# A clustered-attention and MoE kernel: spreading 1/sum over rows by float16 products of two halves, and a planner that holds an engine for shorter waits

## The chip, the core and the metric

The kernel runs on one core of a Trainium2 chip. The core has engines with a queue of their own each: TensorE (PE for the products, PEld for the loading of their stationary operand), VectorE (DVE), ScalarE (ACT), GpSimd (POOL), and SyncE (SP), which issues the transfers here. Each works through its queue in order and waits on semaphores of the others. The metric is the device time of one execution in microseconds (us); less is better.

## The reference

Queries, keys and values of 4 batches, 8 heads, 768 positions and 64 columns. Each query and each key is given to the nearest of 16 centroids of its head, and a query sees only keys of its own cluster. The output of the attention goes through two matrices with a gate between them.

```python
q_assign = np.argmax(np.einsum('bhsd,hcd->bhsc', q_n, c_n), axis=-1)
k_assign = np.argmax(np.einsum('bhsd,hcd->bhsc', k_n, c_n), axis=-1)
mask = q_assign[:, :, :, None] == k_assign[:, :, None, :]
scores = np.where(mask, scale * np.matmul(q, k.transpose(0, 1, 3, 2)), -1000000000.0)
scores = scores - np.max(scores, axis=-1, keepdims=True)
attn = np.exp(scores)
attn = attn / (np.sum(attn, axis=-1, keepdims=True) + 1e-09)
x = np.matmul(attn, v)                       # then (B*S, H*D) = 3072 x 512
h = x @ w_in                                 # 512 x 2048
g = np.where(h >= 1, h, np.where(h <= -1, 0.0, (h + 1) ** 2 / 4))
out = g @ w_out                              # 2048 x 512
```

## The kernel before

Numbers are kept as two float16 halves, a high one and what is left over; a product of two such numbers is three float16 products (high·high, high·low, low·high) that add up in PSUM.

The work is cut into units: a batch, a pair of heads and a chunk of 256 queries, 4 × 4 × 3 = 48 of them. For a unit, `at_scores` runs four times (two heads, two blocks of 128 queries): four products of 384 columns on TensorE into `bank`, and one VectorE instruction that adds a mask value and takes the row's bound into `sS` and `sbi`. `at_soft` takes the exponential on ScalarE with the row sum in `rs`, splits it into the halves `hl` (ScalarE makes the high one, POOL subtracts it for the low one), and SP issues the transpose of `hl` to `pT`. After the fourth (`n == 3`) ScalarE copies the four sums with 1e-9 added, and VectorE takes the reciprocal `rr`.

`at_av` (lines 758 to 791) is one group of instructions on TensorE. It fills one half of the PSUM tile `banka` with 1/sum, each number spread over 64 rows and its query's column: four products of a broadcast column of `rr` with the float32 identity `idf`, 128 columns wide. The other half gets the 36 products of `pT` with the values, 256 columns wide. Both heads of the pair stand side by side: their products use 64 columns of the array each. ScalarE then copies the 1/sum half to `rb`, VectorE multiplies, and ScalarE and POOL split the result into the halves of `x` (in some units the tile's name is `wk`).

`ffn1` and `ffn2` are the two matrix products for 256 rows of x; their steps on the other engines are named `r` and `g`. Ahead of it all, keys, queries and values are loaded, scaled, split and transposed (`kv_scale`, `kq_split`, `v_split`), each batch gets a bound of its values (`v_bound`, `v_am`), centroid products give the clusters (`assign`, products named `<-cT`), and the weights are scaled and split (`w_bits`, `w_sum`, `w_split`; the products `<-wk,ones`).

None of this is issued as it is written. `Recorder` collects all instructions as nodes with their dependencies, and `issue` (line 274) plans the order: `forward` runs a model of the engines with the prices of `price`, `backward` makes priorities from it, eight rounds are made, and the order of the round with the shortest modelled end is issued. Nearly every instruction therefore has line 289 in the profile. In `forward`, an engine normally takes the instruction that is ready and has the best priority. Lines 182 to 188 make the exception: where another instruction becomes ready within `LOOK` times the price of the chosen one, and has a priority better by more than `MARGIN` ns, the engine waits for that.

```python
more = [(s, r, i) for r, s, i in q[:8] if r < t + x.cost * LOOK and s < pick[0] - MARGIN]
if more:
    heappush(avail[e], pick)
    _, t, i = min(more)
```

Of the kernel before, what the change touches and what calls it, by code (L numbers as in the profile page):

```python
# [9 lines left out]
F16 = mybir.dt.float16  # L10
BF16 = mybir.dt.bfloat16
F32 = mybir.dt.float32
U32 = mybir.dt.uint32
AF = mybir.ActivationFunctionType
ALU = mybir.AluOpType
# [5 lines left out]


ONE, ES_MIN = 65504.0, 2.0**-23
EXP_MASK2 = 0x7F000000
TINY = 2.0**-47
W_TINY = 2.0**-90
# [2 lines left out]
LATENCY = dict(tensor=280, scalar=252, vector=230, gpsimd=175)  # L29
COLD, AHEAD = 75e3, 1500  # L30

LOOK, MARGIN = 1.0, 3000
ROUNDS = 8


# [312 lines left out]
def tile_clustered_attention_moe(  # L348
# [10 lines left out]
    nc = tc.nc  # L359
    B, H, S, D = q.shape  # L360
    C = cent.shape[1]
# [4 lines left out]
    P = 128  # L366
    T = S // P
    NP = H // 2
    CT = 2
# [18 lines left out]
    rec = Recorder(tc)  # L388
# [48 lines left out]
    rings["c"] = Ring([rings["sS"].bufs[1][:, i * D : (i + 1) * D] for i in range(3)])  # L437
    rings["c_hl"] = Ring([rings["sS"].bufs[2]])
    make_identity(nc, idf)
    iota = const.tile([P, C], F32, name="iota")  # L440
    for c in range(C):
        nc.gpsimd.memset(iota[:, c : c + 1], float(C - c))
    zero = const.tile([P, 1], F32, name="zero")
    nc.gpsimd.memset(zero, 0.0)
    onh = const.tile([P, P], F16, name="onh")
    nc.gpsimd.memset(onh, 1.0)
    ones = const.tile([P, P], BF16, name="ones")
    nc.gpsimd.memset(ones, 1.0)
    cst = new("c", [D], F32)
# [122 lines left out]
    def assign(b, hp):  # L572

        e = KV[b, hp]
        n2 = 2 * T
        n4 = 2 * n2
        z1 = misc(n4, C)
        for i, x in enumerate("kq"):
            with rec.group():
                for n in range(n2):  # L580
                    h = 2 * hp + n // T
                    for a in range(2):
                        rec.tensor.matmul(
                            z1[:, i * n2 + n],
                            e[x + "T"][:, n],
                            cT[:, a, h * C : (h + 1) * C],
                            start=(a == 0),
                            stop=(a == 1),
                        )
        mx = new("mx", [n4], F32)  # L590

        def wide(x):
            return x.unsqueeze(2).to_broadcast([P, n4, C])


        rec.vector.tensor_reduce(out=mx, in_=z1, op=ALU.max, axis=AX.X)
        rec.vector.tensor_tensor(out=z1, in0=z1, in1=wide(mx), op=ALU.is_equal)
        rec.vector.tensor_tensor(out=z1, in0=z1, in1=iota.unsqueeze(1).to_broadcast([P, n4, C]), op=ALU.mult)
        rec.vector.tensor_reduce(out=mx, in_=z1, op=ALU.max, axis=AX.X)
        rec.vector.tensor_tensor(out=z1, in0=z1, in1=wide(mx), op=ALU.subtract)  # L600

        rec.gpsimd.memset(e["kn"][:, :, 0, C:], 0.0)
        for i, x in enumerate("kq"):
            rec.vector.tensor_scalar(
                out=e[x + "n"][:, :, 0, :C],
                in0=z1[:, i * n2 : (i + 1) * n2],
                scalar1=0.0,
                scalar2=-ONE if x == "k" else ONE,
                op0=ALU.not_equal if x == "k" else ALU.is_equal,
                op1=ALU.mult,  # L610
            )

        kn, qn = e["kn"], e["qn"]
        rec.gpsimd.tensor_tensor(
            out=kn[:, :, 1], in0=kn[:, :, 1], in1=e["phi"].unsqueeze(2).to_broadcast([P, n2, D]), op=ALU.mult
        )
        kf = e["kT"].rearrange("p n q -> p (n q)")
        rec.scalar.activation(out=kf, in_=kf, func=AF.Copy, scale=e["phi"])
        qf = e["q"].rearrange("p j (t d) -> p (j t) d", d=D)
        rec.scalar.activation(out=qn[:, :, 1], in_=qf, func=AF.Copy, scale=e["sc"][:, 1:2])  # L620
        for x, part in (("k", 3), ("q", 2)):
            e[x + "1"] = view(e["parts"][part], [n2, P], F16)
            transpose(e[x + "1"], e[x + "n"])

        pn = misc(2, C)
        with rec.group():
            for t in range(T):
                rec.tensor.matmul(pn, onh, kn[:, t::T, 0, :C], start=(t == 0), stop=(t == T - 1))
        has = new("has", [2, C], F32)
        rec.vector.tensor_scalar(out=has, in0=pn, scalar1=-ONE * (S - 0.5), scalar2=None, op0=ALU.is_gt)  # L630

        zq = z1[:, n2:].rearrange("p (j t) c -> p j t c", j=2)
        rec.vector.tensor_tensor(out=zq, in0=zq, in1=has.unsqueeze(2).to_broadcast([P, 2, T, C]), op=ALU.add)
        zm = z1[:, :n2, 0]
        rec.vector.tensor_reduce(out=zm, in_=z1[:, n2:], op=ALU.max, axis=AX.X)
        er = e["er"] = new("er", [n2], F32, NP)
        rec.vector.tensor_scalar(out=er, in0=zm, scalar1=e["es"], scalar2=None, op0=ALU.mult)
# [97 lines left out]
    def at_soft(b, hp, c, j, t):  # L735
        e = A.setdefault((b, hp, c), {})
        n = j * CT + t
        sS, bi = A.pop((b, hp, c, j, t))
        if n == 0:
            e["rs"] = new("rs", [4], F32, 4)  # L740
        if t == 0:
            e["pT", j] = new("pT", [2 * T, CT, P], F16, 3)
        sf = sS.rearrange("p a s -> p (a s)")
        rec.scalar.activation(
            out=sf, in_=sf, func=AF.Exp, bias=bi, scale=-1.0, accum_out=e["rs"][:, n : n + 1]
        )
        hl = new("hl", [2, S], F16, 3)
        rec.scalar.copy(hl[:, 0], sf)
        rec.gpsimd.tensor_tensor(out=hl[:, 1], in0=sf, in1=hl[:, 0], op=ALU.subtract)
        rec.sync.dma_start_transpose(out=e["pT", j][:, :, t, :], in_=hl.rearrange("p a s -> p (a s)"))  # L750
        if n == 3:

            rr = new("rr", [4], F32, 3)
            rec.scalar.activation(out=rr, in_=e["rs"], func=AF.Copy, bias=1e-9)
            rec.vector.reciprocal(rr, rr)
            e["rr"] = rr

    def at_av(b, hp, c):
        u = b * NCH + c
# [2 lines left out]
        pv, rb = bank_a[:, :CQ], bank_a[:, CQ:]  # L762
        with rec.group():
            for t in range(CT):
                for j in range(2):
                    rec.tensor.matmul(
                        rb[j * D : (j + 1) * D, t * P : (t + 1) * P],
                        e["rr"][:, j * CT + t : j * CT + t + 1].to_broadcast([P, D]),
                        idf,
                        start=True,  # L770
                        stop=True,
                    )
            for kc in range(T):
                for i, (va, pa) in enumerate(((0, 0), (0, 1), (1, 0))):
                    for j in range(2):
                        pT = e["pT", j].rearrange("p (a n) t q -> p a n (t q)", a=2)[:, pa, kc]
                        rec.tensor.matmul(
                            pv[j * D : (j + 1) * D],
                            kv["vs"][:, va, j, kc * D : (kc + 1) * D],
                            pT,  # L780
                            start=(kc == 0 and i == 0),
                            stop=(kc == T - 1 and i == 2),
                        )
# [272 lines left out]
```

## Time and profile before

| | us |
|---|---|
| median of three runs | 966.27 |
| lowest and highest of them | 966.08, 966.28 |
| the execution that was profiled | 964.51 |
| its span, first to last instruction | 962.7 |
| mean granted clock of TensorE | 0.976 |

The profile is of one execution. Its page has the busy time of each engine, the span in 40 slices, the chain of work that ended last, and the costliest groups of instructions. The views that are quoted below also give the timeline of one engine, the groups with their shapes kept apart, the waits by who waited for whom, and busy times in chosen windows. A timeline row has the start, the length, the engine, the source line, the operation, output and inputs, and in brackets the idle time just before it with what ended it. In a group's row stand count, busy time, mean ns of one, and idle time before them.

### The profile page before, as it was taken

The page shows a single profiled execution, that of the slowest core. Times are in us where ns is not written, and L with a number is a line of the kernel's source. Part 1 is how long each engine was busy: PE and PEld are TensorE (multiplying, and loading weights), DVE is VectorE, ACT ScalarE, POOL GpSimd, SP SyncE. Part 2 cuts the span into 40 slices and gives each one's busy share as a digit, 9 for nine tenths or more (in the row PEclk, how much of TensorE's full clock was granted, in tenths as well). Part 3 has the DMA queues.
Part 4 walks back from the last instruction along what each step waited for, and adds up shares of the span by engine and source line. Part 5 has one row for each costly group of instructions (what it writes and reads, how often), then busy time and mean ns, then how long its engine had stood idle before and what let it go on. Part 6 is the DMA issues. An engine that isn't in the chain of part 4 may idle for free.

```text
span 962.7 us, 19220 instructions
## 1 busy us (share of the span) xinstructions
PE 824.1 (86%) x7348; PEld 567.2 (59%) x7348; DVE 639.8 (66%) x1341; ACT 654.8 (68%) x1095; POOL 551.2 (57%) x421
## 2 busy tenths in 40 slices
PE   0335547878999999998988999999989999999998
PEld 0223335555666766675656766776666757767664
DVE  6998986878689865556778665546986554454231
ACT  3676877775667877765767687757777677676332
POOL 1375777574555767663655667656655666656311
PEclk9999779989999999999999999999999999999999
DMA  9998787778589986876789878867999776566100
GB/s 279 263 202 195 175 207 161 164 175 194 125 176 178 169 141 117 170 148 142 173 154 198 145 156 152 166 130 159 209 192 154 139 132 122 108 118 110 34 22 22
DMA packets 426780, 148.68 MB, mean 154 GB/s; under 512 B 403520, under 2 KB 418880, under 8 KB 426688
## 3 DMA queue, kind: packets, MB, share of 16 engines
q1 hardware_dynamic: 426688, 147.46, 75.7%
q8 instruction: 57, 0.93, 0.4%
q14 instruction: 35, 0.29, 0.1%
HBM read 40.40 MB, written 6.29 MB: 49 GB/s over the span
## 4 chain that ended last, share of the span: by engine, by line
PE 67%; DVE 22%; issue 5%; ACT 2%; POOL 2%; DMA 1%; SPq 0%; ACTq 0%; DVEq 0%; POOLq 0%
PE bank L289 47%; PE banka L289 12%; PE bankh L289 9%; DVE w L289 4%; DVE sS L289 4%; DVE bank L289 2%; DVE r L289 2%; DVE wk L289 1%; DVE am L289 1%; DVE qn L289 1%; DVE kn L289 1%; POOL hl L289 1%; DVE kvq L289 1%; DVE mx L289 1%; DMA kvq<-in_v_dram 1%
## 5 line engine op out<-in xcount | busy, mean ns | idle before, releaser
L289 POOL TENSOR_TENSOR hl<-sS,hl 128x768 f16<-128x768 f32 x192 | 330.4, 1725 | 182.5 <-ACT hl L289 103.6
L289 PE MATMUL bank<-w,g 128*128 128x512 f16 x1152 | 273.1, 383 | 0.5 <-DVE o L289 0.5
L289 PEld LDWEIGHTS <-kvq 128*64 128x64 f16 (+1 forms) x3264 | 195.4, 107 | 128.3 <-issue 80.8
L289 PEld LDWEIGHTS <-w 128*128 128x128 f16 x2304 | 224.5, 98 | 66.7 <-issue 25.5
L289 DVE CUSTOM_DVE_ANT_0 sS<-bank,zero,er 128x768 f32<-128x768 f32 x192 | 194.2, 1012 | 93.1 <-PE bank L289 77.0
L289 ACT ACTIVATE sS<-sS,sbi 128x768 f32<-128x768 f32 x192 | 179.2, 933 | 98.8 <-DVE sbi L289 92.8
L289 PE MATMUL bank<-kvq 128*128 128x384 f16 x768 | 164.1, 338 | 47.5 <-DVE sbi L289 42.0
L289 POOL TENSOR_TENSOR g<-r,g 128x512 f16<-128x512 f32 x96 | 115.2, 1200 | 152.7 <-ACT g L289 139.5
L289 PEld LDWEIGHTS <-g 128*128 128x128 f16 x1152 | 111.0, 98 | 122.8 <-issue 10.1
L289 ACT CAST hl<-sS 128x768 f16<-128x768 f32 x192 | 157.4, 825 | 7.4 <-DMA pT<-hl 5.6
L289 PE MATMUL bank<-x,w 128*128 128x256 f16 x1032 | 125.6, 275 | 10.0 <-DVE r L289 4.4
L289 ACT ACTIVATE r<-r,f_ra,f_rs 128x512 f32<-128x512 f32 x96 | 77.8, 811 | 79.4 <-DVE r L289 74.7
L289 PE MATMUL banka<-pT,kvq 128*64 128x256 f16 x1728 | 108.0, 281 | 0.0
L289 DVE TENSOR_SCALAR r<-bank,f_lo,f_hi 128x512 f32<-128x512 f32 x64 | 51.7, 808 | 61.6 <-PE bank L289 45.4
L289 ACT CAST g<-r 128x512 f16<-128x512 f32 x96 | 58.8, 613 | 31.7 <-DVE r L289 24.8
L289 DVE SCALAR_TENSOR_TENSOR r<-bank,f_gs,r 128x512 f32<-128x512 f32 x64 | 48.0, 749 | 30.9 <-ACT r L289 18.7
L289 PE MATMUL bank<-wk,w 128*128 128x256 f16 x504 | 60.1, 272 | 5.9 <-DVE r L289 4.9
L289 PE MATMUL bankh<-x,w 128*128 128x256 f16 x504 | 59.9, 273 | 0.2 <-DVE es L289 0.2
L289 DVE TENSOR_SCALAR r<-bankh,f_lo,f_hi 128x512 f32<-128x512 f32 x32 | 25.9, 809 | 30.8 <-PE bankh L289 24.8
L289 PEld LDWEIGHTS <-ones 128*128 128x128 bf16 x148 | 13.9, 120 | 50.5 <-issue 46.7
L289 POOL TENSOR_TENSOR w<-w 128x1024 f16<-128x1024 f32 x14 | 31.5, 2252 | 14.7 <-ACT w L289 14.7
L289 PE MATMUL bank<-wk,ones 128*128 128x128 bf16 x116 | 13.2, 277 | 29.8 <-DVE wk L289 29.8
(135 smaller groups left out, 840.1 us busy)
## 6 DMA issues: line engine op xcount, KB each, us to landing
w<-in_moe_w_in_dram SPq DMA_DIRECT2D x14, 512.0 KB, 4.9
w<-in_moe_w_out_dram SPq DMA_DIRECT2D x14, 512.0 KB, 4.3
kvq<-in_k_dram SPq DMA_DIRECT2D x16, 384.0 KB, 4.0
kvq<-in_q_dram SPq DMA_DIRECT2D x16, 384.0 KB, 3.7
kvq<-in_v_dram SPq DMA_DIRECT2D x16, 384.0 KB, 4.1
out_dram<-o SPq DMA_DIRECT2D x11, 512.0 KB, 3.4
pT<-hl SPq DMA_TRANSPOSE x192, 4.1
o<-in_v_dram SPq DMA_DIRECT2D x8, 384.0 KB, 3.9
```

The costliest lines, as they stand in the source:

```text
L289: fn(*args, **kw)
```

## The change

1/sum is split into two float16 halves. ScalarE scales the sum by 2^-10 ahead of the reciprocal, in place in `rs`; POOL converts the reciprocal (a CAST to `rr`) and subtracts (the second half of `rr`). `at_av` has eight float16 products where it had four of float32: high and low half after one another into the same place. Their moving operand is `idu`, an identity that is scaled by 2^-10, made once on POOL. The ones of float16 (`onh`) go, and `assign` uses those of bfloat16. In the planner LOOK goes from 1.0 to 0.4 and MARGIN from 3000 to 4000.

```diff
+UNIT = 2.0**-10
...
-LOOK, MARGIN = 1.0, 3000
+LOOK, MARGIN = 0.4, 4000
...
     make_identity(nc, idf)
+    idu = const.tile([P, P], F16, name="idu")
+    rec.gpsimd.tensor_scalar(out=idu, in0=idf, scalar1=UNIT, scalar2=None, op0=ALU.mult)
...
-    onh = const.tile([P, P], F16, name="onh")
-    nc.gpsimd.memset(onh, 1.0)
...
-                rec.tensor.matmul(pn, onh, kn[:, t::T, 0, :C], start=(t == 0), stop=(t == T - 1))
+                rec.tensor.matmul(pn, ones, kn[:, t::T, 0, :C], start=(t == 0), stop=(t == T - 1))
...
-            rr = new("rr", [4], F32, 3)
-            rec.scalar.activation(out=rr, in_=e["rs"], func=AF.Copy, bias=1e-9)
+            rr = e["rs"]
+            rec.scalar.activation(out=rr, in_=rr, func=AF.Copy, scale=UNIT, bias=1e-9 * UNIT)
             rec.vector.reciprocal(rr, rr)
-            e["rr"] = rr
+            rh = e["rr"] = new("rr", [2, 4], F16, 3)
+            rec.gpsimd.tensor_copy(rh[:, 0], rr)
+            rec.gpsimd.tensor_tensor(out=rh[:, 1], in0=rr, in1=rh[:, 0], op=ALU.subtract)
...
-                for j in range(2):
-                    rec.tensor.matmul(
-                        rb[j * D : (j + 1) * D, t * P : (t + 1) * P],
-                        e["rr"][:, j * CT + t : j * CT + t + 1].to_broadcast([P, D]),
-                        idf,
-                        start=True,
-                        stop=True,
-                    )
+                for a in range(2):
+                    for j in range(2):
+                        n = j * CT + t
+                        rec.tensor.matmul(
+                            rb[j * D : (j + 1) * D, t * P : (t + 1) * P],
+                            e["rr"][:, a, n : n + 1].to_broadcast([P, D]),
+                            idu,
+                            start=(a == 0),
+                            stop=(a == 1),
+                        )
```

The order changes on all five queues. Three places follow. The first is POOL in the 43rd unit, where its third and fourth `hl` are made. `hl` are the halves of the exponentials, `x` the split output, `g` the split gate; before:

```order
L289 TENSOR_TENSOR g_213<-r_212,g_213 128x512
L289 TENSOR_TENSOR hl_170<-sS_78,hl_170 128x768
L289 TENSOR_TENSOR x_68<-rb_176,x_68 128x256
L289 TENSOR_TENSOR hl_171<-sS_79,hl_171 128x768
L289 TENSOR_TENSOR g_214<-r_212,g_214 128x512
```

and in the changed kernel:

```order
L290 TENSOR_TENSOR hl_171<-sS_77,hl_171 128x768
L290 TENSOR_TENSOR hl_169<-sS_78,hl_169 128x768
L290 CAST rr_172<-rs_164 128x4
L290 TENSOR_TENSOR rr_172<-rs_164,rr_172 128x4
L290 TENSOR_TENSOR x_68<-rb_175,x_68 128x256
L290 TENSOR_TENSOR hl_170<-sS_79,hl_170 128x768
L290 TENSOR_TENSOR g_213<-r_211,g_213 128x512
```

The conversion and the subtraction of 1/sum now stand between the unit's fourth `hl` and the `x` of an earlier unit.

The second place is VectorE at the start of the program, where the maxima of keys and queries (`am`), those of the values (`v_am`) and the first low halves (`kn`, `qn`) are made; `kvq_61` to `kvq_64` are the four head pairs of the first batch. Before:

```order
L289 TENSOR_REDUCE v_am_129<-kvq_62 128x1
L289 RECIPROCAL sc_133<-bankh 128x2
L289 TENSOR_SCALAR bankh<-bankh 128x1
L289 TENSOR_REDUCE v_am_129<-kvq_63 128x1
L289 TENSOR_SCALAR es_135<-bankh 128x1
L289 SCALAR_TENSOR_TENSOR kn_139<-kvq_61,sc_133,kn_139 128x12x64
L289 SCALAR_TENSOR_TENSOR qn_141<-kvq_61,sc_133,qn_141 128x12x64
L289 TENSOR_REDUCE v_am_129<-kvq_64 128x1
L289 TENSOR_REDUCE am_132<-kvq_62 128x2
```

and in the changed kernel:

```order
L290 RECIPROCAL sc_132<-bankh 128x2
L290 TENSOR_SCALAR bankh<-bankh 128x1
L290 TENSOR_REDUCE am_131<-kvq_62 128x2
L290 TENSOR_REDUCE v_am_128<-kvq_62 128x1
L290 SCALAR_TENSOR_TENSOR kn_138<-kvq_61,sc_132,kn_138 128x12x64
L290 TENSOR_REDUCE v_am_128<-kvq_63 128x1
L290 TENSOR_SCALAR es_134<-bankh 128x1
L290 SCALAR_TENSOR_TENSOR qn_140<-kvq_61,sc_132,qn_140 128x12x64
L290 TENSOR_REDUCE v_am_128<-kvq_64 128x1
```

The maximum of the second head pair's keys and queries has moved from behind all four maxima of the values to ahead of the second one. On SP, the load of the fourth pair's values has moved from the eighth to the eleventh place.

The third place is TensorE near the start, between the centroid products of the first head pair (`<-cT`) and the first sum over weights (`<-wk,ones`). Before:

```order
L289 LDWEIGHTS kvq_61
L289 MATMUL bank_74<-cT,kvq_61 128x16
L289 LDWEIGHTS ones
L289 MATMUL bank_74<-am_131,ones 128x2
L289 LDWEIGHTS ones
L289 MATMUL bank_73<-wk_66,ones 128x128
```

and in the changed kernel:

```order
L290 LDWEIGHTS ones
L290 MATMUL bank_73<-wk_66,ones 128x128
L290 LDWEIGHTS ones
L290 MATMUL bank_74<-am_130,ones 128x2
L290 LDWEIGHTS kvq_61
L290 MATMUL bank_74<-cT,kvq_61 128x16
```

Before, both groups of centroid products of the pair come ahead of the sum over the weights; now the sum stands between the first group and the second.

## The prediction

> **What bounds the kernel now.** I began with the head of the page, the slices and the chain that ended last.
>
> ```profile
> span 962.7 us, 19220 instructions
> PE 824.1 (86%) x7348; PEld 567.2 (59%) x7348; DVE 639.8 (66%) x1341; ACT 654.8 (68%) x1095; POOL 551.2 (57%) x421
> PE   0335547878999999998988999999989999999998
> PEclk9999779989999999999999999999999999999999
> PE 67%; DVE 22%; issue 5%; ACT 2%; POOL 2%; DMA 1%; SPq 0%; ACTq 0%; DVEq 0%; POOLq 0%
> PE bank L289 47%; PE banka L289 12%; PE bankh L289 9%; DVE w L289 4%; DVE sS L289 4%; DVE bank L289 2%; DVE r L289 2%; DVE wk L289 1%; DVE am L289 1%; DVE qn L289 1%; DVE kn L289 1%; POOL hl L289 1%; DVE kvq L289 1%; DVE mx L289 1%; DMA kvq<-in_v_dram 1%
> ```
>
> The row of PE digits falls into two programs. Through the first dozen slices (about 24 us each) TensorE works three to eight tenths of the time; from there to the end it is full. The chain says the same: two thirds of the span is matmul work, and nearly all that is left is VectorE. POOL holds 2%. The windows give the two parts their sizes, the second view those of the product with the scaled identity (x288 is 36 blocks of eight records).
>
> ```profile
> 0.00:300.00 300.00, 189.09 (x1771) 130.19 (x1772) 247.63 (x549) 207.75 (x323) 176.60 (x142) 0.94 0.84 191
> 300.00:963.00 663.00, 635.00 (x5579) 437.06 (x5576) 392.13 (x793) 447.03 (x773) 374.55 (x280) 0.99 0.72 138
> 300.00:963.00 663.00, 23.65 (x288) 14.96 (x288) 0.00 (x0) 0.99 0.72 138
> ```
>
> The columns are length, then PE, PEld, DVE, ACT and POOL, the granted clock, DMA. After 300 us TensorE is idle for 663 − 635 = 28 us and no other engine is busy for more than 447 of 663. There a nanosecond taken from TensorE is a nanosecond of span as long as no other wait moves in. Before 300 us TensorE has 111 us idle, and VectorE (248 of 300) is the engine in front.
>
> **The float32 products.** Each at_av block (48 of them: 4 batches, 4 head pairs, 3 query chunks) begins with four float32 products that spread 1/sum over 64 rows each. Two blocks in the timeline, columns start and length, one at the full clock, one early at a low clock:
>
> ```profile
> 463.50 0.66 PE L289 MATMUL banka<-idf,rr 128*64 128x128 f32 x8
> 463.99 2.13 PE L289 MATMUL banka<-pT,kvq 128*64 128x256 f16 x36
> 466.05 0.50 PE L289 MATMUL bank<-wk,w 128*128 128x256 f16 x3
> 145.01 1.12 PE L289 MATMUL banka<-idf,rr 128*64 128x128 f32 x8
> 145.92 0.42 PE L289 MATMUL banka<-pT,kvq 128*64 128x256 f16 x2
> ```
>
> Lengths overlap, so I take starts. Four float32 products leave eight records and hold TensorE from 463.50 to 463.99, 0.49 us. The 36 float16 products behind them, 256 columns wide, take 463.99 to 466.05, 2.06 us; as they go in pairs (two column halves of the array side by side), that is 0.114 per pair. So a float32 pair of 128 columns costs what a float16 pair of 256 columns costs: four of those are 0.44, and 0.05 is the start of the block. The new block has eight float16 products of 128 columns, four pairs again, each half as wide: 4 × 0.057 + 0.05 = 0.28. The saving is **0.21 us** a block at the full clock. In the cold block the old part takes 145.01 to 145.92, 0.91 us, and half of nearly all of it would go, 0.42.
>
> What could spoil this is the loading of weights, since there are still two loads in each pair.
>
> ```profile
> L289 PEld LDWEIGHTS <-kvq 128*64 128x64 f16 x1728 | 98.9, 114 | 1.6
> L289 PEld LDWEIGHTS <-kvq 128*128 128x128 f16 x1536 | 96.5, 99 | 126.6 <-issue 80.8 <-DMA kvq<-kn 2.0 <-DMA kvq<-qn 1.0
> L289 PEld LDWEIGHTS banka<-idf,rr 128*64 128x64 f32 x384 | 21.5, 144 | 17.2 <-issue 10.0 <-DVE rr L289 4.3 <-ACT hl L289 1.5
> 462.22 1.25 PEld L289 LDWEIGHTS <-kvq 128*128 128x128 f16 x47
> ```
>
> A load's record (mean 99 to 144 ns) is mostly latency: 47 full loads start within 1.25 us, (1.25 − 0.10)/46 = 25 ns apart. Loads of 64 columns are slower in the record than those of 128 (114 against 99), and float32 ones slower again (144); yet two of these slowest ones already fit into a pair of 0.11 us. The difference of 30 ns between float32 and float16 is about half of a 55 ns share of that pair, so I take a float16 load as 25 to 30 ns, and two fit into 0.057. Ends: at 25 ns for each of eight products the block is 0.25 and the saving 0.24; if loads set the pace at the old one, the saving is 0. I take 0.21, which lies near the upper end because the stream of 25 ns loads is the nearest row.
>
> The Trainium skill speaks against the change here. "TensorE: Matmul & The Clock Gate", section "LDWEIGHTS (loading the stationary operand)", gives a load as columns divided by 1.2 in ns, 53 for 64 columns, and "TensorEngine Tiling (Array Packing)", under "Restrictions" of its modes, says that column tiling turns the fast weight load off; by an estimate from that page two loads, one after the other, would take 0.107 per pair, the block would stay at 0.48, and the sum below would lose its first term. The trace does not decide it, because every pair of 64-column products in it is 0.11 long anyway. What the case without a gain would give is worked out as a rival below.
>
> Sum for TensorE: 36 blocks after 300 us × 0.21 = 7.6. Of the 12 earlier blocks some run at 0.91 and some at 0.49; I take 0.3 each, and count half, because TensorE is busy 189 of 300 there: 12 × 0.3 / 2 = 1.8. Together **−9.4 us**; ends 0 and −12 (0.24 × 36 + 0.3 × 12).
>
> **The two new POOL instructions.** The halves of 1/sum are made on POOL: 96 instructions on 4 elements. The nearest rows:
>
> ```profile
> 144.99 0.18 POOL L289 COPY w_all<-w_iw 128x2 f32<-128x2 f32 x1 [2.01 <-DVE w_iw L289]
> 145.51 1.65 POOL L289 TENSOR_TENSOR hl<-sS,hl 128x768 f16<-128x768 f32 x1 [0.34 <-POOL w_all L289]
> 816.92 0.67 POOL L289 TENSOR_TENSOR x<-rb,x 128x256 f16<-128x256 f32 x1
> ```
>
> A copy of two elements takes 0.18. A subtraction takes 1.65 at 768 and 0.67 at 256 columns, a slope of 1.9 ns and 0.18 at no width, so 0.19 at four. The pair is 0.37 without gaps and 1.05 with a gap like the 0.34 shown at both ends; I take 0.5, or 24 us in all. POOL is idle for 963 − 551 = 412 us. The cover, in one unit: 1/sum at the top, the last subtraction before the transposes, the PE block:
>
> ```profile
> 815.10 0.20 ACT L289 ACTIVATE rr<-rs 128x4 f32<-128x4 f32 x1
> 815.32 1.64 POOL L289 TENSOR_TENSOR hl<-sS,hl 128x768 f16<-128x768 f32 x1 [1.70 <-ACT rr L289]
> 816.47 0.17 DVE L289 RECIPROCAL rr<-rr 128x4 f32<-128x4 f32 x1
> 824.44 0.66 PE L289 MATMUL banka<-idf,rr 128*64 128x128 f32 x8
> pT<-hl SPq DMA_TRANSPOSE x192, 4.1
> ```
>
> The block starts 7.8 us after the reciprocal ends (816.64). Its real partner is the transpose: hl is ready at 816.96 and 4.1 more make 821.1, so 3.3 us are spare. In the changed order the conversion and its subtraction stand just behind this hl and delay the x and hl subtractions that follow by 0.5. Behind a delayed POOL, VectorE waits for free buffers.
>
> ```profile
> DVE r L289 <- POOL g L289: 19.6, 13, 2.0
> DVE sS L289 <- POOL hl L289: 11.9, 10, 2.1
> ```
>
> These 31.5 us grow with POOL's load, by 24/551 = 4.4%: **+1.4 us**. Ends: 0, since all spare time covers it, and +24 if nothing did. The latter is a rival. The ScalarE step has a scale added but the same count; the VectorE reciprocal stays; one 128-column conversion at the start is long done at 85 us, when the first block runs. The ones of bfloat16 for those of float16 leave counts and shapes as they are. These count nothing.
>
> **The order.** With LOOK at 0.4 the planner holds an engine only for shorter waits. All five queues come out in another order, while units and counts stay. Two stretches of equal length and like work show what order and its waits are worth:
>
> ```profile
> 300.00:400.00 100.00, 98.93 (x866) 67.84 (x864) 68.16 (x142) 75.91 (x136) 63.33 (x48) 1.00 0.86 158
> 400.00:500.00 100.00, 91.08 (x817) 62.41 (x816) 66.05 (x123) 65.91 (x110) 54.10 (x42) 0.98 0.72 150
> PE bank L289 <- DVE sbi L289: 35.2, 21, 3.4
> PE bank L289 <- DVE wk L289: 29.8, 12, 6.4
> 8.22 0.96 DVE L289 TENSOR_REDUCE v_am<-kvq 128x1 bf16<-128x768 f32 x1 [0.79 <-DMA kvq<-in_v_dram]
> 10.27 0.95 DVE L289 TENSOR_REDUCE v_am<-kvq 128x1 bf16<-128x768 f32 x1 [0.76 <-DMA kvq<-in_v_dram]
> ```
>
> TensorE idles 1.1 us in the one and 8.9 in the other (where a new batch is prepared): 7.8 us. The two wait rows are those of TensorE before 300 us, for the scores' buffer and for the weights' bits. The first pieces of VectorE show the direction: it waited 0.79 and 0.76 for V loads, and the new order puts a maximum of keys and queries into that gap, but moves the load of the fourth V behind others on SP. Some of it wins and some loses. I take 0, with ends of −8 and +8 from the two windows.
>
> **Sum.** −9.4 + 1.4 + 0 = −8.0. The span is 962.7 and the execution that was profiled took 964.5, 1.8 more (both are in the table of times), so it becomes 956.5. The median of the three runs, 966.3, lies 1.8 above that execution: **958.3 us**, 0.8% less. What a measurement of this kernel can tell from no change is about 0.2%, 1.9 us.
>
> **Rivals.**
> - *The order gains as well.* −8.0 and another −8: 950. For it: 111 us of idle TensorE before 300 us. Against: those waits go to VectorE, whose work is the same.
> - *The order loses what the products gain.* −8.0 + 8 = 0: 966. The new queue puts TensorE's sum over the first weights ahead of the second group of centroid products, which then waits with it for VectorE's weight bits; one such wait took up to 6.4 us (last column above).
> - *The products gain nothing*, because loads set the pace of a pair: +1.4, 967.7. For it: 114 against 99 ns for fewer columns. Against: two float32 loads fit in 0.11.
> - *POOL stands still at the head of its queue*, and the kernel is slower. The conversion waits for VectorE's reciprocal, and everything on POOL waits behind it, hl for the next transposes above all. In the unit above the reciprocal came 1.2 us after ScalarE was done (815.30 to 816.47); from 3.3 us of stall on, TensorE waits. A stall of 3.8 in each of the 36 late units would cost 36 × 0.5 = 18: 958.3 + 18 = 976. Against: in the new order the conversion mostly stands behind the unit's fourth hl, when the reciprocal is due.
>
> **How the numbers follow.** Chances: forecast (952 to 964) 0.58, order gains 0.14, order loses 0.12, no gain of the products 0.08, POOL stalls 0.08. Of the third, a third each falls to faster, same and slower; the fourth gives 0.03 to same. So faster 0.76, same 0.07, slower 0.17, with 964.3 and 968.2 as the borders. The ends of all terms together reach 946 (−12 − 8) and far above 976; leaving out the stalling POOL and the last of the better orders, I set **948 to 969**.
>
> **What would show it.** Right: eight float16 records per block, with the next product 0.28 us after the first; TensorE's identity windows after 300 us halved; POOL's busy time up by 18 to 24 us and its share of the chain still at a few per cent; the same 28 us of idle TensorE after 300 us. Wrong: the start of the pT products still 0.45 or more behind (loads); waits of POOL's conversion for VectorE's reciprocal that are longer than 3 us, and TensorE waiting for pT or rr (POOL); TensorE idle before 300 us far from 111 (order). If the block shrinks but the idle after 300 us grows by as much, another engine has taken the pace.

## The result, and the profile after

| | before | after |
|---|---|---|
| median, four executions each (us) | 966.27 | 941.20 |
| lowest and highest | 966.08, 967.06 | 940.61, 941.30 |
| the execution that was profiled | 964.51 | 940.61 |
| its span | 962.7 | 938.8 |
| mean granted clock of TensorE | 0.976 | 0.955 |

The changed kernel takes 0.9738 of the time before (95% interval 0.9721 to 0.9755): 25 us less where 8 were forecast, and 7 below the lower end of the range. The sign was right, the size was not. The head of the page of the changed kernel:

```profile
span 938.8 us, 19265 instructions
...
PE 805.3 (86%) x7348; PEld 552.9 (59%) x7348; DVE 637.9 (68%) x1341; ACT 652.6 (70%) x1095; POOL 567.5 (60%) x517
...
PE   1334455889998999999997999999989999999998
...
PEclk9957666999999999999999999999999999999999
```

Compare the digits of PE with those before. The two programs are still there, but the full one begins a slice sooner. A faster TensorE clock is no explanation in the rise: from the third to the seventh slice the granted clock is lower than before (5 to 7 tenths against 7 to 9). Only after 300 us is it a little higher (1.00 against 0.99 in the windows); what that is worth is read from the stretches further down. TensorE is busy for 18.8 us less (824.1 to 805.3) and idle for 5.1 less (138.6 to 133.5). The chain of waits on this page breaks off after 15% of the span, so it is not read here. The same windows as before, with the end moved to the new end:

```profile
0.00:300.00 300.00, 191.74 (x1835) 131.37 (x1836) 255.05 (x565) 212.34 (x331) 187.96 (x172) 0.86 0.87 195
300.00:939.00 639.00, 613.59 (x5517) 421.49 (x5513) 382.84 (x777) 440.28 (x765) 379.55 (x346) 1.00 0.74 141
```

and the second of them for the products with the scaled identity alone:

```profile
300.00:939.00 639.00, 14.88 (x288) 0.00 (x0) 1.00 0.74 141
```

In the first 300 us TensorE gets through 64 matmul records more than before (1835 against 1771) at a lower clock, with idle time nearly unchanged (108 against 111). After 300 us it is idle for 25 us, where it was 28. By these windows alone the order seems to have done little. They mislead, because they cut two different programs at the same clock time. A landmark in the work is better, and the identity blocks are one: 48 of them, 12 to a batch. The timeline's rows for the 12th, 24th, 36th and 48th of the kernel before:

```profile
291.61 0.66 PE L289 MATMUL banka<-idf,rr 128*64 128x128 f32 x8
...
508.74 0.66 PE L289 MATMUL banka<-idf,rr 128*64 128x128 f32 x8
...
710.16 0.66 PE L289 MATMUL banka<-idf,rr 128*64 128x128 f32 x8
...
900.88 0.66 PE L289 MATMUL banka<-idf,rr 128*64 128x128 f32 x8
```

and of the changed kernel:

```profile
283.83 0.41 PE L290 MATMUL banka<-idu,rr 128*64 128x128 f16 x8
...
489.09 0.41 PE L290 MATMUL banka<-idu,rr 128*64 128x128 f16 x8
...
690.41 0.41 PE L290 MATMUL banka<-idu,rr 128*64 128x128 f16 x8
...
877.19 0.41 PE L290 MATMUL banka<-idu,rr 128*64 128x128 f16 x8
```

The lead is 7.8 us at the 12th block, 19.7 at the 24th, 19.8 at the 36th and 23.7 at the 48th. Half of it is made between the 12th and the 24th, a stretch to which the prediction gave no term of its own. The experiments below are read with the same landmark.

### The profile page after: what moved, and what is told of

It reads as the page before. It is cut to its first block, busy times and chain, and to the rows that moved or that the text cites. A ratio compares the mean times of both kernels' runs of the same rounds, so it can differ in the third digit from the quotient of the medians.

```text
span 938.8 us, 19265 instructions
## 1 busy us (share of the span) xinstructions
PE 805.3 (86%) x7348; PEld 552.9 (59%) x7348; DVE 637.9 (68%) x1341; ACT 652.6 (70%) x1095; POOL 567.5 (60%) x517
## 5 line engine op out<-in xcount | busy, mean ns | idle before, releaser
L290 PEld LDWEIGHTS <-kvq 128*64 128x64 f16 (+1 forms) x3264 | 191.6, 106 | 121.7 <-issue 74.8
L290 POOL TENSOR_TENSOR g<-r,g 128x512 f16<-128x512 f32 x96 | 112.4, 1170 | 128.0 <-ACT g L290 125.6
L290 PE MATMUL banka<-pT,kvq 128*64 128x256 f16 x1728 | 106.1, 278 | 0.8 <-DMA pT<-hl 0.8
L290 PEld LDWEIGHTS <-ones 128*128 128x128 bf16 x244 | 18.6, 113 | 59.3 <-issue 53.8
```

Source lines behind the costliest of these rows:

```text
L290: fn(*args, **kw)
```

## The experiments

### Products and order apart

e1 has the new products, and on TensorE, VectorE, ScalarE and SyncE exactly the order of before; POOL's two instructions are put in where the reciprocal is due. e2 is the other half: float32 products in exactly the order of the changed kernel, with POOL's pair still made but not used. e11 is e2 without the pair.

```diff
 e1, against the changed kernel
-LOOK, MARGIN = 0.4, 4000
+LOOK, MARGIN = 1.0, 3000
+            rec.open.cost += 4 * (512 / 4.8 + 1.2) - 8 * (128 / 4.8 + 1.2)
...
+        self.nodes = [x for x in every if not x.extra]
...
+            self.order.insert(at, x)
```

```diff
 e2, against the changed kernel
-                            e["rr"][:, a, n : n + 1].to_broadcast([P, D]),
-                            idu,
+                        e["rs"][:, n : n + 1].to_broadcast([P, D]),
+                        idf,
...
+            rec.open.cost += 8 * (128 / 4.8 + 1.2) - 4 * (512 / 4.8 + 1.2)
```

```diff
 e11, against e2 (after each of the two POOL instructions)
+            rec.nodes[-1].calls = []
```

> The float16 products with the order of before held fast on PE, VectorE, ScalarE and SP; on POOL the two new instructions stand at the place where the reciprocal is due. Theory 'two parts that add': the products are worth the 10 us that the blocks lose (20.9 to 10.6 us of TensorE work) and the order the other 14, so 954 to 957 us. Rival 'they need each other' (the shorter blocks only pay in an order planned for them): 960 to 966. Rival 'the order is worth nothing by itself; shorter blocks bring everything forward': 940 to 945.

> The float32 products with the order of the changed kernel held fast on all five queues; the two POOL instructions are kept, but their result is not used. Theory 'two parts that add': 951 to 954 us. Rival 'they need each other': 960 or more. Rival 'shorter blocks bring everything': 964 to 968.

> e2 without the two POOL instructions per unit, everything else in its place: what these cost. By the prediction's step (+1.4): 950 to 951 us against 952 of e2. Rival 'nothing': 952. Rival 'POOL's waits for the reciprocal reach TensorE': 944 to 948.

Measured, medians: e1 955.15 us (0.9887 of before, 0.9838 to 0.9936), e2 952.03 (0.985, 0.9812 to 0.9889), e11 953.24 (0.9879, 0.9848 to 0.991). Products alone are worth 11 us in the old order (966 to 955) and 11 in the new one (952 to 941); the order alone 14 with either kind of product. The two parts add up. (With the repeats e11, e15 and e17 in their place the order comes to 12 to 17.) Without POOL's pair the kernel is no faster, so the pair costs nothing that these runs can tell (the intervals of e2 and e11 overlap). e1 was timed once more, as e17 below, at 958.39; with it the products in the old order come to 7 to 11 us.

The table gives the start of the 12th identity block, the steps from there to the 24th, 36th and 48th, and from the 48th to the end of the span, each from the timeline of one profiled execution (us).

| kernel | to 12th | 12th to 24th | 24th to 36th | 36th to 48th | to the end |
|---|---|---|---|---|---|
| before | 291.6 | 217.1 | 201.4 | 190.7 | 61.8 |
| e1: products, old order | 291.0 | 215.2 | 198.7 | 188.5 | 61.6 |
| e17: e1 again | 293.6 | 215.2 | 198.7 | 188.6 | 61.6 |
| e2: float32, new order | 283.2 | 207.9 | 204.2 | 189.7 | 61.9 |
| e11: e2 without the pair | 286.9 | 208.0 | 204.3 | 189.7 | 61.9 |
| changed kernel | 283.8 | 205.3 | 201.3 | 186.8 | 61.6 |
| e15: changed kernel again (below) | 284.0 | 205.4 | 203.0 | 186.8 | 61.6 |

e1 and e17 are the same kernel. They agree within 0.2 us in every stretch after the 12th block and differ by 2.6 before it; e2 and e11 differ by 3.7 there, so what is read from the first stretch is not firm. The later stretches repeat, with one exception: in e15 the third is 1.7 us longer than in the other execution of the changed kernel. The same twelve products take longer in e15 (second row):

```profile
512.78 1.47 PE L290 MATMUL bank<-x,w 128*128 128x256 f16 x12
...
513.02 2.66 PE L290 MATMUL bank<-x,w 128*128 128x256 f16 x12
```

TensorE's granted clock drops to half there. One of the kernel before, in a window of 2 us (the clock, 0.50, is the third number from the end; the windows on both sides have 0.91 and 0.74):

```profile
490.00:492.00 2.00, 2.00 (x6) 0.76 (x5) 1.97 (x3) 0.79 (x3) 1.64 (x1) 0.50 0.02 4
```

Added up over the three windows, 1.7 us of TensorE's time are lost, as much as 3.4 us at half the clock. Before, e1 and e17 each have one such drop in the second and one in the last of the three later stretches; e2, e11 and the changed kernel have none there, and e15 has one. In these executions 3.4 us of what the order is worth are therefore clock. Whether the order keeps the clock up was not tried; e15 shows that one and the same order can have a drop or not.

The new products take 1.9 to 2.9 us from each later stretch. The new order takes some 7 us from the first stretch (4.7 to 9.8, by which executions are compared) and 9 to 10 from the second, 1.7 of them a drop of the clock; it gives 2.6 to 2.8 back in the third, and takes 1 to 2 from the last, no more than the drop there. The stretches do not hold quite the same work: by the 12th block the new order has run 21 matmul records more than the old one, by the 24th 21 fewer. In the third the changed kernel has its longest wait of TensorE after 300 us, and e15 has the same one just ahead of its drop:

```profile
512.08 0.81 PE L290 MATMUL bank<-kvq 128*128 128x384 f16 x4 [3.74 <-DVE sbi L290]
```

### Is it the shorter holding?

The prediction treated LOOK as what it says, less holding. If that were the cause, time should follow the number.

```diff
 e3, against the changed kernel (e5 to e8 and e12 likewise, with the numbers of the table)
-LOOK, MARGIN = 0.4, 4000
+LOOK, MARGIN = 1.0, 3000
```

```diff
 e4, against the kernel before
-LOOK, MARGIN = 1.0, 3000
+LOOK, MARGIN = 0.4, 4000
```

> The float16 products planned anew with LOOK 1.0 and MARGIN 3000, which the planner prices as shorter. Theory 'shorter holds are what the order gains by': as e1, 953 to 958 us. Rival 'any new plan is a new draw and this one was lucky': anywhere from 938 to 962, and not near e1 in particular.

> The kernel before with LOOK 0.4 and MARGIN 4000 alone, planned anew; no new POOL instructions. Theory 'shorter holds are what the order gains by': 949 to 955 us. Rival 'a draw': anywhere from 945 to 972.

> The changed kernel with LOOK 0 (MARGIN 4000): the planner never holds an engine. Its work is the changed kernel's. Theory 'shorter holds are the gain': at or below LOOK 0.4, 936 to 943 us. Rival 'a draw': anywhere from 938 to 962. Third view, 'some holds are worth having': 943 to 950, above LOOK 0.4.

> The changed kernel with LOOK 0.2: 95 holds instead of 209. Theory 'shorter holds': 937 to 943 us, between LOOK 0 and LOOK 0.4. Rival 'a draw': no order among the values, 938 to 962.

> The changed kernel with LOOK 0.6: 237 holds. Theory 'shorter holds': between LOOK 0.4 and LOOK 1.0 (955), 943 to 951 us. Rival 'a draw': 938 to 962, perhaps below LOOK 0.4.

> The changed kernel with MARGIN back at 3000 and LOOK at 0.4: 196 holds against 209, none of them long. Theory 'shorter holds': as the changed kernel, 938 to 944 us. Rival 'a draw': a plan that differs in small things lands elsewhere, up to 955.

> The changed kernel with LOOK 0.45 and MARGIN 4500, a near neighbour in both numbers. If the two numbers as such made the gain: 940 to 943 us. If each plan is a draw: anywhere from 941 to 957.

| products | LOOK, MARGIN | median (us) | ratio to before, interval |
|---|---|---|---|
| float16 (e5) | 0, 4000 | 962.65 | 0.9973 (0.9954 to 0.9992) |
| float16 (e6) | 0.2, 4000 | 958.07 | 0.992 (0.989 to 0.995) |
| float16 (e8) | 0.4, 3000 | 953.7 | 0.9885 (0.986 to 0.991) |
| float16 (changed kernel) | 0.4, 4000 | 941.2 | 0.9738 (0.9721 to 0.9755) |
| float16 (e12) | 0.45, 4500 | 951.18 | 0.9853 (0.9823 to 0.9882) |
| float16 (e7) | 0.6, 4000 | 947.9 | 0.9822 (0.98 to 0.9843) |
| float16 (e3) | 1.0, 3000 | 954.65 | 0.9883 (0.9846 to 0.992) |
| float32 (e4) | 0.4, 4000 | 961.54 | 0.9958 (0.9935 to 0.998) |

The time does not follow the number. A MARGIN of 3000 for 4000 loses 12 us, a little more of both loses 10, and float32 products planned with the same two numbers gain 4.5 and not 14. Each setting gives another order, and the orders lie up to 21 us apart on the same work. The changed kernel's is the best of the seven; that shorter holds are better is not shown, and between 0.2 and 1.0 it is not even a trend. The changed kernel was also timed once more (e15), on another chip:

> The changed kernel as it is, beside e13 and e14. If the first measurement holds on this chip: 939 to 943 us. If part of the 941 was the chip: 944 to 948.

It took 942.94 us, 0.9778 of before (0.9749 to 0.9806).

### Where the order gains

Four kernels follow one order up to the 12th or 24th identity block and the other for the rest, all with float16 products.

```diff
 e9, against the changed kernel (e13 with CUT = 24; e10 and e14 with a, b = (old, new))
+        a, b = (new, old)
+        n, k = 0, 0
+        while n < CUT:
+            n += a[k].more > 0
+            k += 1
+        done = set(a[: k - 1])
+        self.order = a[: k - 1] + [x for x in b if x not in done]
```

> Float16 products; the new order up to the twelfth at_av block (about 280 us), the old order of e1 for all that is left. By the idle time of TensorE the new order is ahead by 10 to 11 us at that place and by 5 to 6 more behind it. Theory 'most of the order's gain is made where the last weights and the second batch are prepared beside the first gate products': 944 to 947 us. Rival 'it comes bit by bit over the whole program': 950 to 952.

> The other half: float16 products, the old order up to the twelfth at_av block, the new order behind it. Theory 'most of the gain is early': 949 to 952 us, and e9 and e10 together give the whole (955 less 14). Rival 'the later part is worth as much or more': 943 to 947.

> Float16 products; the new order up to the 24th at_av block (about 520 us), the old order behind it. Theory 'the gain lies in the ramp and in the preparing of the second batch': 940 to 945 us, nearly the whole. Rival 'it needs the whole order': 948 to 953, as with the cut at 12.

> Float16 products; the old order up to the 24th block, the new one behind it. Theory 'ramp and second batch': 952 to 956 us, as e1. Rival 'the gain comes over the whole program': 946 to 950.

| kernel | median (us) | to 12th | 12th to 24th | 24th to 36th | 36th to 48th |
|---|---|---|---|---|---|
| e9: new to the 12th, then old | 951.12 | 286.8 | 213.7 | 198.7 | 188.7 |
| e10: old to the 12th, then new | 954.21 | 294.6 | 204.1 | 204.3 | 186.8 |
| e13: new to the 24th, then old | 941.24 | 283.9 | 205.9 | 199.3 | 188.3 |
| e14: old to the 24th, then new | 959.33 | 288.1 | 215.6 | 204.0 | 187.1 |

The cut at the 24th block is clean: the new order up to there has the whole gain, the new order after it has none. The cut at the 12th is not. By medians its halves gain 4 and 1 us over e1, where the whole gains 14. The second stretch behaves as it should (213.7 with the old order, 204.1 with the new). Why the sum fails is not shown. e9 reaches the 12th block 3 us later than the changed kernel, but e11, in which no orders are joined, does so too. The third stretch takes 204 us where the new order follows the old one (e10, e14); 3.4 us of it in e10 and 1.7 in e14 are drops of the granted clock, and without them 200.9 and 202.3 are left, near the 201.3 of the changed kernel. What the seam itself costs was not tried.

### One kind of place, tried by itself

What do the 10 us of the second stretch consist of? From e1 to the changed kernel TensorE is busy in it for 5.5 us less (203.4 to 197.9): a drop of the clock, and 42 of 1912 matmul records that run in other stretches. It is idle for 4.5 less (11.8 to 7.4), and nearly all of that are waits for VectorE's `r`, the gate step: 7.6 us in e1, 3.4 in the changed kernel. The longest one before, a row of TensorE with the wait in brackets, is this:

```profile
449.51 0.81 PE L289 MATMUL bank<-kvq 128*128 128x384 f16 x4
453.78 2.45 PE L289 MATMUL bank<-wk,w 128*128 128x256 f16 x21 [3.46 <-DVE r L289]
```

VectorE at the same time, before:

```profile
447.86 1.01 DVE L289 CUSTOM_DVE_ANT_0 sS<-bank,zero,er 128x768 f32<-128x768 f32 x1
448.79 0.09 DVE L289 DVE_READ_ACCUMULATOR2_ANT sbi<- 128x1 f32 x1
448.79 1.91 DVE L289 SCALAR_TENSOR_TENSOR kn<-kvq,sc,kn 128x768 f16<-128x768 f32 x1
450.62 2.39 DVE L289 SCALAR_TENSOR_TENSOR qn<-kvq,sc,qn 128x768 f16<-128x768 f32 x1
452.93 0.80 DVE L289 TENSOR_SCALAR r<-bank,f_lo,f_hi 128x512 f32<-128x512 f32 x1
```

and POOL, before:

```profile
448.72 1.15 POOL L289 TENSOR_TENSOR g<-r,g 128x512 f16<-128x512 f32 x1 [5.89 <-ACT g L289]
449.84 2.35 POOL L289 TENSOR_TENSOR hl<-sS,hl 128x768 f16<-128x768 f32 x1
```

Read the three together. TensorE has nothing to do from 450.3 on, because `r` has to empty a buffer first. `r` stands on VectorE behind the low halves of keys and queries, `kn` and `qn`, for which TensorE does not wait there. And these two take 1.91 and 2.39 us there, while the same two instructions take 1.01 each in the changed kernel:

```profile
439.38 1.01 DVE L290 SCALAR_TENSOR_TENSOR kn<-kvq,sc,kn 128x768 f16<-128x768 f32 x1
440.31 1.01 DVE L290 SCALAR_TENSOR_TENSOR qn<-kvq,sc,qn 128x768 f16<-128x768 f32 x1
442.42 0.81 DVE L290 TENSOR_SCALAR r<-bank,f_lo,f_hi 128x512 f32<-128x512 f32 x1 [1.10 <-PE bank L290]
```

The excess fits POOL: `kn` starts 0.07 after POOL's `g`, and 1.91 is the rest of `g` (to 449.87) and 1.01 more, within 0.2; `qn` starts while `hl` runs and ends 0.8 after it. In the changed kernel `kn` starts as POOL's `g` ends (439.42), and `qn` starts 0.33 ahead of `hl`, so that here POOL is the one that takes longer:

```profile
440.64 2.18 POOL L290 TENSOR_TENSOR hl<-sS,hl 128x768 f16<-128x768 f32 x1 [1.22 <-ACT hl L290]
```

There `r` waits for TensorE and not the reverse, and TensorE's longest wait for `r` just behind it is 0.97. The Trainium skill, "SBUF — State Buffer", section "SBUF: two separate sides", describes such a pair: VectorE operations with two inputs in SBUF and GpSimd operations take turns at one port pair, and whoever comes second is blocked for the whole of the other's instruction. The rows here agree with that (1.01 alone or first, 1.91 and 2.39 behind POOL).

e16 is e1 with one local edit: at the six places of the old order where one such split stands just ahead of `r` (at the place above it is `qn`, while `kn` stays), `r` goes first. e17 is e1 again, beside it on the same chip. e18 makes the same edit in the changed kernel's own order, which has 13 such places.

```diff
 e16, against e1 (e18 the same, against the changed kernel)
+            if not y.gate or k == g:
+                continue
+            at = {x: i for i, x in enumerate(self.order)}
+            for x in reversed(vec[k:g]):
+                if any(x in z.preds for z in self.order[at[x] : at[y] + 1]):
+                    continue
+                self.order.remove(x)
+                self.order.insert(self.order.index(y) + 1, x)
```

> Float16 products in the order of before (as e1), with one local edit of that order: at six places VectorE takes the gate step r ahead of the low half of queries or values (one split of 768 columns) that stood just before it. Theory A, the order's gain sits at such places, where a split on VectorE stands ahead of a step that TensorE waits for: in the second batch's preparation, where TensorE waited 3.46 us for r behind two splits of 1.9 and 2.4 us, the wait falls to about 1.2; the stretch from the 12th to the 24th identity block falls from 215.2 us to about 213; the whole kernel is 2 to 6 us faster than e1. Theory B, the wait only moves (the delayed split makes its transpose and the centroid products late): the first wait falls, but the stretch stays within 1 us of 215.2 and the time within 1 us of e1.

> The kernel of e1 once more, beside e16 on the same chip: 955 by both theories, with 215 us from the 12th to the 24th identity block.

> The changed kernel with the edit of e16 on its own order, which has 13 such places: VectorE takes the gate step r ahead of the splits that stood just before it. If a split ahead of r costs TensorE time wherever it stands, the kernel falls by 2 to 5 us, to 936 to 939. If it costs only where TensorE had come to the end of its own work (the changed order has one wait of 0.97 us for r between 380 and 500 us, where the one before has 3.46), nothing is gained, and VectorE loses time where r is not yet ready and the split would have run: 941 to 946.

| kernel | median (us) | lowest, highest | to 12th | 12th to 24th | 24th to 36th | 36th to 48th |
|---|---|---|---|---|---|---|
| e16 | 953.27 | 951.92, 954.49 | 289.2 | 213.2 | 200.0 | 188.2 |
| e17 | 958.39 | 955.29, 959.47 | 293.6 | 215.2 | 198.7 | 188.6 |
| e18 | 947.6 | 946.85, 948.86 | 285.8 | 207.0 | 202.4 | 188.7 |

The place in e16, VectorE and then TensorE:

```profile
445.76 1.91 DVE L326 SCALAR_TENSOR_TENSOR kn<-kvq,sc,kn 128x768 f16<-128x768 f32 x1
447.59 0.80 DVE L326 TENSOR_SCALAR r<-bank,f_lo,f_hi 128x512 f32<-128x512 f32 x1
448.31 1.67 DVE L326 SCALAR_TENSOR_TENSOR qn<-kvq,sc,qn 128x768 f16<-128x768 f32 x1
```

```profile
446.48 0.81 PE L326 MATMUL bank<-kvq 128*128 128x384 f16 x4
448.44 2.78 PE L326 MATMUL bank<-wk,w 128*128 128x256 f16 x24 [1.15 <-DVE r L326]
```

The wait falls from 3.46 to 1.15 us and the stretch by 2.0, both as theory A said, and the kernel is 5.1 us faster than e17, with no execution of the one in the range of the other. Against e1, the same kernel as e17 on another chip (955.15, from 952.87 to 958.04), it is 1.9, and the ranges overlap. The traces do not bear theory A out. TensorE's waits in the second stretch, first of e17, then of e16 (total, times, longest):

```profile
PE bank L311 <- DVE r L311: 7.6, 5, 3.5
PE bank L311 <- DVE mx L311: 0.2, 1, 0.2
...
PE bank L326 <- DVE r L326: 4.5, 5, 1.2
PE bank L326 <- DVE mx L326: 1.3, 1, 1.3
PE bank L326 <- DVE bank L326: 1.3, 1, 1.3
```

The waits for `r` lose 3.1 us and those for later steps of VectorE gain nearly as much. TensorE is idle in this stretch for 11.8 us in e17 and 11.3 in e16, and in the whole span for 139.9 in both. The other 1.5 of the 2.0 are a drop of the clock that e17 has and e16 has not; the same twelve products:

```profile
489.70 4.44 PE L311 MATMUL bank<-w,g 128*128 128x512 f16 x12
...
484.52 2.75 PE L326 MATMUL bank<-w,g 128*128 128x512 f16 x12
```

Of e16's lead of 4.4 us at the 12th block, 2.9 are there at the 10th (246.31 against 249.24), ahead of the first of the six places. The stretch from the 24th to the 36th block gave 1.3 us back. So the wait moved, as theory B said, and that the swaps gain anything is not shown. Whether they kept the clock up, or e16 was lucky in it, is open.

The same swap in the changed order, e18, costs 4.7 to 6.4 us (947.6 against 942.9 and 941.2). At the place above, `r` in the changed order finds TensorE not done yet (the 1.10 in its row); put first, it makes VectorE stop with the split behind it. VectorE's waits of `r` for TensorE (total, times, longest), in the changed kernel:

```profile
DVE r L290 <- PE bank L290: 60.0, 38, 4.5
...
DVE r L290 <- PE bankh L290: 12.9, 12, 2.8
```

and in e18:

```profile
DVE r L303 <- PE bank L303: 64.5, 37, 4.5
...
DVE r L303 <- PE bankh L303: 16.2, 15, 2.8
```

They grow by 7.8 us, and TensorE's idle time from the 12th block to the 48th by 3.5 (20.3 to 23.7). The loss of time is spread, 1 to 2 us in each of the four stretches of the changed kernel's trace, and no single wait of TensorE shows it. It is also above the 941 to 946 that I gave for that case. No kernel of this study is faster than the changed one; e13 equals it.

## Why the prediction was wrong

**The order.** This step failed: "Some of it wins and some loses. I take 0, with ends of −8 and +8 from the two windows." It was worth −14. Two things were wrong in it. The ends came from one comparison of two windows of 100 us, 7.8 us, while the program has four such preparations, and before them the long rise in which TensorE is idle for 111 us. The rise alone gave some 7 (4.7 to 9.8), the second batch 9 to 10, and the third and fourth together gave 1 to 2 back; 8 was a bound for one place, used for the whole. (3.4 us of the order's part are drops of the clock, a term that the prediction does not have.) And the rival that had the right sign, "the order gains as well", at 950, was given only 0.14 with the argument that "those waits go to VectorE, whose work is the same". VectorE's work is the same (639.8 and 637.9 us busy), and yet, with the same products, TensorE is idle for 7.0 us less (140.5 in e1, 133.5 in the changed kernel): the same work does not mean the same waits. Which places of the order give this stays open; the one kind that was tried left the idle time of e16 where it was. The size is also luck: the two planner numbers gave the best of seven plans, and six other pairs of numbers gave 948 to 963.

**The products.** Right, with a term somewhat too small. An early block of the changed kernel, and what follows the one at 489.09 that is shown above:

```profile
181.17 0.41 PE L290 MATMUL banka<-idu,rr 128*64 128x128 f16 x8
181.42 2.13 PE L290 MATMUL banka<-pT,kvq 128*64 128x256 f16 x36
...
489.34 2.13 PE L290 MATMUL banka<-pT,kvq 128*64 128x256 f16 x36
```

and the group of the loads of these blocks (count, busy time, mean ns of one, idle time before):

```profile
L290 PEld LDWEIGHTS <-rr 128*64 128x64 f16 x384 | 12.7, 112 | 13.4 <-issue 11.6 <-POOL rr L290 0.8 <-POOL hl L290 0.6
```

From 489.09 to 489.34 and from 181.17 to 181.42 it is 0.25 us to the `pT` products, where I took 0.28 and gave 0.25 as the end at which a load takes 25 ns. The saving is 0.24, not 0.21. In the whole kernel −9.4 became −7 to −11 by medians, and by the spans of the profiled executions −7.8 (962.7 to 954.9, e1), −5.0 (to 957.7, e17) and −8.1 (946.9 to 938.8).

**The loads.** The rival in which they set the pace fell: that block would have stayed at 0.48. The load records do not get shorter than those of other 64-column loads (112 ns against 113 for those of `pT`'s products), but they lie over one another. All eight loads of the block at 489.09 lie within 0.25 us, two to a pair of about 0.05:

```profile
489.09 0.25 PEld L290 LDWEIGHTS <-rr 128*64 128x64 f16 x8
```

So the rule that the prediction weighed from the Trainium skill, "TensorE: Matmul & The Clock Gate", section "LDWEIGHTS (loading the stationary operand)", 53 ns for a load of 64 columns, does not hold for these blocks as the spacing of loads. By an estimate from that page eight such loads, one after the other, would be 0.42 us; the whole block took 0.25.

**The windows of the identity.** I said they would be halved; they fell from 23.65 to 14.88. Starts halve, 0.49 to 0.25, while the busy time of a row holds the latency of its last product as well. That was my slip in choosing the sign, not one of the mechanism.

**POOL.** Right in price, a little too high in effect. The pair and the waits of the changed kernel:

```profile
825.37 0.19 POOL L290 CAST rr<-rs 128x4 f16<-128x4 f32 x1
825.63 0.20 POOL L290 TENSOR_TENSOR rr<-rs,rr 128x4 f16<-128x4 f32 x1
```

```profile
POOL rr L290 <- DVE rs L290: 19.2, 14, 2.8
DVE sS L290 <- POOL hl L290: 23.2, 15, 3.5
DVE r L290 <- POOL g L290: 12.8, 9, 2.0
```

The pair takes 0.46 from start to end (0.5 forecast), and POOL is busy for 16.3 us more (567.5 − 551.2; 18 to 24 forecast). POOL does wait for the reciprocal at the head of its queue, 14 times, which was the mechanism of the slow rival, but never longer than 2.8 us, below the 3.3 at which it was to decide. VectorE's waits for `hl` and `g` grew from 31.5 to 36.0, in another order as well; e11 against e2 shows none of it in the time. The +1.4 was 0 within what these runs resolve.

**The signs I set for the order.** "The same 28 us of idle TensorE after 300" came out at 25, and "far from 111" before 300 at 108: both read as if the order had done nothing. Two reasons. The windows cut at the clock, not at the work; by block 12 the changed kernel was already 7.8 us ahead. And with the same products TensorE is busy for 9.1 us less in the new order than in the old (805.3 against 814.4 in e1; the repeats e15 and e17 have 809.5 and 817.8), although its work is the same. Of these, 3.4 are the two drops of the clock after 300 us. A stop of TensorE may cost busy time in the records too, since the row of the eight products above is 0.41 long where the next starts after 0.25; how much that makes was not tried.

## What to carry to other kernels

When a change replans an order, give the order a range of its own, taken from every place at which the bounding engine waits, not from one pair of windows: here seven plans of the same work lay up to 21 us apart, twice what the intended saving was worth. Compare two orders by landmarks in the work (the start of the n-th block), since windows at the same clock time hide the shift. A long wait of the bounding engine can be traced to what stands ahead of its releaser in the other queue, and swapped there by itself. Then compare that engine's idle time and granted clock, and not only the wait or the median: here the wait fell by 2.3 us, the median by 5.1, and the idle time not at all. The same swap elsewhere cost about 5.

## What the runs showed of the hardware

The same VectorE instruction, two inputs of 768 columns in SBUF, took 1.01 us alone or ahead of POOL and 1.91 and 2.39 us behind it. POOL's subtraction of 768 columns, 1.65 us elsewhere, took 2.35 and 2.18 where it met them. The prediction used means and did not see this price.

Eight loads of 64 float16 columns with eight products of 128 columns take 0.25 us, four pairs and their start, with load records of 112 ns each: the record of a load is not the time that the next one has to wait.

TensorE's granted clock can drop to half for about 3.4 us in the middle of full work, which costs 1.7 us: 12 products of 512 columns took 4.44 us in e17 and 2.75 in e16. The same kernel had such a drop in one execution (e15) and not in another.

Two executions of one kernel repeat to 0.2 us from one landmark to the next once TensorE is full, but for these drops, and can differ by 2.6 us in the rise before it (e1 and e17). A local edit is therefore read from its own stretch, with the clock beside it.
